# Block-sparse attention and an MLP on one core: a batch's last tile as one sparse and one dense unit, and the first chunk's down-projection in fp32

## The chip, the cores and the metric

The kernel runs on one core of a Trainium2 chip. A core has five engines that run side by side, each with its own list of instructions: TensorE (PE, matmuls; its weight loads are PEld), VectorE (DVE), ScalarE (ACT), GpSimd (POOL), and SyncE (SP), which issues DMAs. The metric is the device time in microseconds of one execution; the median of several runs is compared.

## What is computed

The reference is a block-sparse attention with a two-layer perceptron behind it, in fp32:

```python
scale = 1.0 / np.sqrt(D)
scores = scale * np.matmul(q, k.transpose(0, 1, 3, 2))
...
mask = np.abs(blk_i - blk_j) <= window
mask = mask | (blk_i == 0) | (blk_j == 0) | (blk_i == n_blocks - 1) | (blk_j == n_blocks - 1)
for qb in range(n_blocks):
    for kb in sampled_blocks[qb]:
        mask[qb * block:(qb + 1) * block, kb * block:(kb + 1) * block] = True
scores = np.where(mask, scores, -1000000000.0)
...
attn = attn / (np.sum(attn, axis=-1, keepdims=True) + 1e-09)
return np.matmul(attn, v).astype(np.float32)
...
h = x @ w_in
g = np.maximum(h, 0.0) + alpha * np.minimum(h, 0.0)
return (g @ w_out).astype(np.float32)
```

There are 4 batches, 8 heads, 768 tokens and 64 columns a head (D), so x has 3072 tokens of 512; w_in is 512 x 2048. `window` is 1, and three blocks are sampled for each of 24. A block is 32 tokens. A row of blocks 1 to 22 attends to at most eight blocks: itself and its neighbours, the first and the last, and three sampled ones. Rows of blocks 0 and 23 attend to all 24.

## The kernel before

**Numbers.** fp32 operands are split into a high and a low fp16 part, and a product is three fp16 matmuls (high x high, high x low, low x high). An fp32 matmul on unsplit operands gives the same product in one instruction that leaves two records in the trace. The weights come from memory as 64-bit numbers and are unpacked by bit operations on VectorE and ScalarE (`emit_n1`, `emit_n2`, `emit_n3`, L1151 to L1165) into fp32, 16 parts of w_in and 16 of w_out. Then squares on TensorE (`emit_w_sq`, L1175) and their diagonal (`emit_w_diag`, by `diag`, L547) give a scale, and `split` (L1274) makes the two fp16 parts: the high one by `times` (L451 on ScalarE), the low one by `rest` (L459 on VectorE, L461 and L462 on GpSimd). For the first five parts of w_out (`W_PE = 5`) the low part is made on TensorE instead (`emit_w_lo_pe`, L1237 and L1238) and copied out.

**Attention.** A batch has six query tiles of 128 rows, shifted by one block: tile t holds blocks 4t+1 to 4t+4, and the last one, t = TS = 5, blocks 21, 22, 23 and 0. The eight heads are two head sets of four. A unit u = (batch, tile, head set) is the work of one tile for one set. A *sparse* unit gathers its sampled keys (`emit_kr`, copies on GpSimd, L735) and values (`emit_vr`, indirect DMAs that GpSimd issues, L696), computes scores (`emit_s`), subtracts the maximum on VectorE (`emit_bias`, L822), takes exponentials on ScalarE, splits the probabilities, has them transposed by DMA from SyncE (`emit_p_t`, L872), and multiplies them by the values (`emit_av`). A *dense* unit takes all 768 keys: per head two halves of 384 (`emit_s_dense`) and 18 value matmuls (`emit_av_dense`). All matmuls of both kinds go through the helper `mm`, L740. Tiles 0 to 4 are sparse in both units, tile 5 is dense in both, because blocks 23 and 0 are in it. The tile's result is scaled, split (`emit_x_hi`, `emit_x_lo`) and transposed by one DMA (`emit_x_t`, L899) into `x`.

**The perceptron** takes chunks of 256 tokens, M0 to M11, three per batch. A chunk is eight up steps (`emit_up`, L1351, 24 fp16 matmuls of 256 columns), each with an activation on VectorE (`emit_act`, L1361 and L1365), a cast (`emit_gh`, L1374) and a low part (`emit_gl`, L1380), and eight down steps (`emit_down`, L1401, 12 fp16 matmuls of 512 columns). M0's up steps are fp32 on unsplit w_in (`emit_up32`, L1339), so that they need only the unpacked weights; its down steps use the split w_out.

**The order.** Every step is an operation of a plan, numbered as it is made. A list `ORDER` names all of them with a letter for the engine (P, D, A, G, S), and `Plan.run` emits them in just that order; dependencies without a semaphore then hold each engine to it. So each engine runs its list in order, and waits where an operand is late.

## Time and profile before

| | |
|---|---|
| median of 3 runs | 772.27 us (769.94 to 779.11) |
| profiled execution | 771.31 us, span 769.1 us, granted clock 0.982 |
| TensorE busy | 700.2 us, 91% |
| VectorE busy | 535.7 us, 70% |
| GpSimd busy | 483.1 us, 63% |
| ScalarE busy | 371.9 us, 48% |
| first and last matmul of the perceptron | 103.8 us, end at 764.6 us |

The span runs from the first to the last instruction of the profiled execution; 2.2 us of its time lie outside. "Busy" is the time in which an engine has at least one instruction under way. Granted clock is TensorE's, as a share of full speed. A label such as L740 is a line of the kernel, and for a helper all its callers share it.

### The profile page before, as it was taken

Reading aid. Unit: us, or ns where it says so; the run is one execution under the profiler, and the core shown is the slowest. Engines: PE = TensorE matmul, PEld = TensorE weight load, DVE = VectorE, ACT = ScalarE, POOL = GpSimd, SP = SyncE. Lnnn points to the kernel's source line nnn. Section 1 sums busy time; section 2 is a strip of 40 time slices with the busy share of each in tenths; the row PEclk is TensorE's granted clock in tenths of the full one; section 3 lists DMA queues with packets and bytes.
Section 4 is the critical chain, followed back from the end, with each engine's and each line's share of the span. In section 5 each row is a group of like instructions: output and inputs, shape, how many; then the busy total and the mean of one; then the engine's idle time right before and its main releaser. Section 6 shows DMA issues by size and latency. Waiting matters only on the chain.

```text
span 769.1 us, 25326 instructions
## 1 busy us (share of the span) xinstructions
PE 700.2 (91%) x9978; PEld 493.2 (64%) x9978; DVE 535.7 (70%) x1377; ACT 371.9 (48%) x838; POOL 483.1 (63%) x849
## 2 busy tenths in 40 slices
...
GB/s 180 326 276 208 204 171 236 164 178 144 163 185 227 173 200 201 207 202 194 174 197 197 208 182 218 186 188 172 185 213 199 150 155 162 167 99 113 65 1 29
DMA packets 284599, 136.49 MB, mean 177 GB/s; under 512 B 216992, under 2 KB 272304, under 8 KB 284480
## 3 DMA queue, kind: packets, MB, share of 16 engines
...
## 4 chain that ended last, share of the span: by engine, by line
PE 60%; DVE 16%; DMA 9%; issue 4%; POOL 4%; ACT 3%; SPq 2%; POOLq 0%; ACTq 0%; DVEq 0%
PE o L1401 24%; PE h L1351 23%; PE s L740 6%; PE a L740 5%; DMA pt<-ph 3%; DMA qs<-qt 3%; DVE ph L459 2%; DVE e L822 2%; POOL gl L1380 1%; DMA wo<-in_moe_w_in_dram 1%; DMA rawp<-in_sampled_blocks_dram 1%; DVE g L1361 1%; DVE wi L1165 1%; ACT rawp L447 1%; DVE wo L1165 1%
## 5 line engine op out<-in xcount | busy, mean ns | idle before, releaser
L1351 PE MATMUL h<-x,wi 128*128 128x256 f16 x2112 | 240.2, 273 | 0.7 <-DVE g L1365 0.7
L1351 PEld LDWEIGHTS <-wi 128*128 128x128 f16 x2112 | 204.7, 98 | 31.4 <-issue 2.2
L1401 PE MATMUL o<-wo,gh 128*128 128x512 f16 x728 | 219.7, 384 | 0.5 <-ACT g L1411 0.5
L1380 POOL TENSOR_TENSOR gl<-g,gh 128x512 f16<-128x512 f32 x91 | 110.5, 1221 | 90.6 <-ACT gh L1374 77.8
L735 POOL COPY keys<-keys 128x128 f16 x480 | 133.4, 327 | 20.6 <-ACT keys L604 16.1
L1401 PE MATMUL o<-wo,gl 128*128 128x512 f16 x364 | 139.7, 384 | 0.0
L829 ACT ACTIVATE e<-e,nm 128x256 f32<-128x256 f32 x160 | 79.9, 500 | 107.8 <-DVE nm L822 96.8
L1361 DVE SCALAR_TENSOR_TENSOR g<-h,am 128x512 f32<-128x512 f32 x96 | 65.9, 687 | 77.3 <-PE h L1351 57.0
L1401 PEld LDWEIGHTS <-gh 128*128 128x128 f16 x728 | 69.4, 99 | 77.8 <-issue 6.1
L1374 ACT CAST gh<-g 128x512 f16<-128x512 f32 x91 | 55.4, 611 | 105.1 <-DVE g L1365 57.6
L696 POOL DMA_INDIRECT vr<-scr,vidx x80 | 81.3, 1016 | 25.3 <-issue 19.8
L822 DVE CUSTOM_DVE_ANT_0 e<-s,bias,cs 128x256 f32<-128x256 f32 x160 | 73.5, 478 | 29.3 <-POOL ph L462 13.8
L1365 DVE SCALAR_TENSOR_TENSOR g<-h,gsc,g 128x512 f32<-128x512 f32 x96 | 72.1, 751 | 3.4
L740 PEld LDWEIGHTS <-pt 128*32 128x32 f16 (+1 forms) x4416 | 57.6, 96 | 25.0 <-issue 12.9
L740 PE MATMUL s<-keys,qs 128*32 128x192 f16 (+2 forms) x864 | 70.1, 255 | 2.9 <-DMA qs<-qt 2.9
L740 PE MATMUL s<-keys,qt 128*32 128x192 f16 (+2 forms) x864 | 69.4, 256 | 3.3 <-DVE nm L822 1.7
L1401 PEld LDWEIGHTS <-gl 128*128 128x128 f16 x364 | 35.9, 99 | 44.0 <-issue 1.9
L461 POOL TENSOR_SCALAR e<-e 128x512 f32<-128x512 f32 (+1 forms) x38 | 28.2, 742 | 57.1 <-ACT ph L451 24.8
L459 DVE SCALAR_TENSOR_TENSOR ph<-e,ph 128x512 f16<-128x512 f32 (+1 forms) x62 | 60.1, 975 | 4.2 <-ACT ph L451 3.7
L462 POOL TENSOR_TENSOR ph<-e,ph 128x512 f16<-128x512 f32 (+1 forms) x38 | 50.4, 1326 | 3.2
L451 ACT ACTIVATE ph<-e 128x512 f16<-128x512 f32 (+1 forms) x69 | 47.7, 693 | 9.3 <-DMA pt<-ph 8.1
L836 DVE CUSTOM_DVE_ANT_0 e<-s,dbias,cs 128x384 f32<-128x384 f32 x64 | 38.0, 612 | 11.2 <-PE s L740 8.1
...
## 6 DMA issues: line engine op xcount, KB each, us to landing
...
```

The lines of the kernel that those rows point to most:

```text
L459: nc.vector.scalar_tensor_tensor(dst, src, scale, hi, ALU.mult, ALU.subtract)
L696: nc.gpsimd.indirect_dma_start(dst[:n], None, T["scr", b].rearrange("s h a -> s (h a)"), bass.IndirectOffsetOnAxis(ap=vidx[:n, i : i + 1], ...
L735: nc.gpsimd.tensor_copy(kr[:, :, g, r], kt[:, :, bass.ds(i * HB2, HB2)])
L740: nc.tensor.matmul(dst, lhs, rhs, start=start, stop=False, skip_group_check=True)
L822: nc.vector.tensor_tensor_reduce(e_view(u, h // 2)[:, h % 2, :], T["sp", u, h], bias[:, t], scale=T["cs", b, t][:, c : c + 1], scalar=3.0e ...
L829: nc.scalar.activation(e, e, AF.Exp, bias=T["nm", u, h], scale=-1.0, accum_out=su_of(u, h))
L1351: nc.tensor.matmul(ph[:, i, :], win(k, f, ct), x[:, l, ct, cols], start=(m == 0), stop=(m == len(terms) - 1))
L1361: nc.vector.scalar_tensor_tensor(g, ph, 0.0, a2, ALU.min, ALU.mult)
L1365: nc.vector.scalar_tensor_tensor(g[:, i : i + 2], ph[:, i : i + 2], sc, g[:, i : i + 2], ALU.mult, ALU.add)
L1374: nc.scalar.copy(T["gh", c, j, half], g)
L1380: nc.gpsimd.tensor_tensor(T["gl", c, j, half], g, T["gh", c, j, half], ALU.subtract)
L1401: nc.tensor.matmul(T["o", c, t], g[:, i, a : a + P], wout(w, f), start=(f == 0 and m == 0), stop=(f == NF - 1 and m == 2),)
```

## The change

A batch's last tile becomes one sparse and one dense unit. Blocks 21 and 22 of all eight heads make the sparse one: rows 0 to 63 of the tile are the two blocks for the first head set, rows 64 to 127 the same blocks for the second. Blocks 23 and 0 of all eight heads make the dense one, in the same way. So the queries are loaded by six DMAs instead of two, scaled in two halves, and each dense matmul of 128 query rows becomes two of 64, one for each head set, that write different halves of the partitions (`row_sets`). `emit_x_t` puts the last tile back together with four transposes instead of one. The dense mask goes, since rows of blocks 23 and 0 attend to everything.

M0's down-projection becomes fp32 on unsplit w_out (`emit_down32`), in the order of steps 7 to 0, on the activations as they are: without `emit_gh` and `emit_gl` for that chunk. It needs the unpacked parts of w_out, and neither their scale nor their split. The split of w_out now stands behind these down steps, part by part, and all its low parts are made on VectorE or GpSimd. `ORDER` is a new list.

```diff
-W_PE = 5
...
-S289 S274 S26 A307 S272 S273 A308 D309 A312 D313 P12 D13 S290 G0 D1 D4 A8 S359 D27 A28 G2 S14 P275 D276 D277 P278 D279 S291 P314 P316 D29 A42 D317 S74
...
+S268 A269 D270 S251 A273 S250 D274 G0 D1 S25 S252 S193 S37 S194 S195 S29 D26 D27 D28 S17 S235 P253 D254 D255 D4 P277 A278 A9 D38 S233 D39 S320 A5 P256
...
+    NSB = NBLK - 2
+    HR = P // 2
...
     def emit_load_q(e, b, t):
         T["qf", b, t] = wt("qf", [P, H, D], F32)
+        if t == TS:
+            first = TS * P + BLK
+            for c in range(NQ):
+                hs = slice(c * HQ, (c + 1) * HQ)
+                for a, z, v, s in ((0, HR, 0, first), (0, BLK, 1, S - BLK), (BLK, HR, 1, 0)):
+                    load(e, T["qf", b, t][c * HR + a : c * HR + z, v * HQ : (v + 1) * HQ], q_tok[b][s : s + z - a, hs])
+            return
         for a, z, s in q_rows(b, t):
...
-    def picks(eng, t, use):
-        for i in range(NG4 * NR):
-            use(i // NR, i % NR, idx[eng][NG4 * NR * t + i])
+    def lay(u, g):
+        b, t, c = units[u]
+        return (c, g) if t < TS else (g // 2, g % 2)
+
+    def cs_of(u):
+        b, t, c = units[u]
+        return (c,) if t < TS else tuple(range(NQ))
...
+    def row_sets(u):
+        b, t, c = units[u]
+        return [(c, slice(0, P))] if t < TS else [(x, slice(x * HR, (x + 1) * HR)) for x in range(NQ)]
...
     def emit_s_dense(u, h, z):
-        b, t, c = units[u]
+        b, t, w = units[u]
         T["sp", u, h, z] = sp = wt("s", [P, 512], F32)
-        kt = T["kt", b, c][:, h, z]
         for x, key in enumerate(("qt", "qs")):
-            mm(sp[:, :CP], T[key, b, t][:, c * HQ + h, :], kt, x == 0)
+            for c, r in row_sets(u):
+                mm(sp[r, :CP], T[key, b, t][:, w * HQ + h, r], T["kt", b, c][:, h, z], x == 0)
...
     def emit_av_dense(u, h):
         b, t, c = units[u]
-        av = av_of(u) if h == 0 else T["av", b, t]
+        av = T["av", b, t]
         for i in range(NT):
-            av_mm(av[:, c * HQ + h], T["pt", u, h, i // 3], i % 3, v_tile(b, c, i, h), (c, h, i) == (0, 0, 0))
+            for x, y in TERMS:
+                for q, r in row_sets(u):
+                    mm(av[r, c * HQ + h], T["pt", u, h, i // 3][:, 3 * x + i % 3, r], v_tile(b, q, i, h)[:, y * D : (y + 1) * D], False)
...
+    def is_dense(u):
+        return units[u][1:] == (TS, 1)
...
     def emit_x_t(b, t):
         cc = chunks.index((b, t // 2))
         if ("x", cc) not in T:
             T["x", cc] = wt("x", [P, 2 * NC, W2], F16)
-        nc.sync.dma_start_transpose(
-            T["x", cc][:, :, (t % 2) * P : (t % 2 + 1) * P], T["xn", b, t].rearrange("p a c -> p (a c)")
-        )
+        x, xn = T["x", cc], T["xn", b, t]
+        if t < TS:
+            nc.sync.dma_start_transpose(x[:, :, (t % 2) * P : (t % 2 + 1) * P], xn.rearrange("p c l x -> p (c l x)"))
+            return
+        for w in range(2):
+            for c in range(NQ):
+                at = P + w * HR
+                nc.sync.dma_start_transpose(
+                    x[:, c * NC : (c + 1) * NC, at : at + HR], xn[c * HR : (c + 1) * HR, w * NC // 2 : (w + 1) * NC // 2].rearrange("p c l x -> p (c l x)")
+                )
 
...
-    def emit_w_lo_pe(name, f):
-        w, hi, lo, s = wparts(name, f)
-        T["d", name, f] = wt("o", [P, 512], F32)
-        nc.tensor.matmul(T["d", name, f], T["sid", f // 2 if name == "wi" else NG], w, start=True, stop=False)
-        nc.tensor.matmul(T["d", name, f], nident, hi, start=False, stop=True)
...
+    def split_all(name, o_w, free):
             if f == NF // 2:
                 prev = None
-            held = [o_al, o_pack] if f == 0 else []
-            prev, o_wi[f] = split("wi", f, 0, [gs[f // 2], ups[f // 2]] + held, prev, False, None, None)
+            prev = o_w[f] = split(name, f, free(f), prev)
...
+    def emit_down32(j):
+        if j == NG - 1:
+            for t in range(2):
+                T["o", 0, t] = wt("o", [P, DM], F32)
+        for i in range(2):
+            for t in range(2):
+                nc.tensor.matmul(
+                    T["o", 0, t], T["g", 0, j, None][:, i, t * P : (t + 1) * P], wo[:, 2 * j + i + 1, :],
+                    start=(j == NG - 1 and i == 0), stop=(j == 0 and i == 1),
+                )
...
+    def g_pool(c, j):
+        return "vf" if c == 0 and j < NG - bufs["g"] else "g"
...
-            sc = gsc[:, f : f + 1] if c else gsc0
+            sc = gsc[:, f : f + 1] if c else 1.0
...
+        if c == 0:
+            items = [("u", j) for j in range(ng)] + [("d", j) for j in reversed(range(ng))]
...
+                if c == 0:
+                    gh[j] = o
+                    continue
...
+            elif c == 0:
+                d = [gh[j]] + [raw_wo[n * j + i] for i in range(n)] + downs[-1:]
+                downs.append(plan.op(p, {"PE": 3.45}, lambda j=j: emit_down32(j), d, [] if downs else obufs, [gb[j]] + (obufs if downs else [])))
...
-            split_wi(ups)
+            split_all("wi", o_wi, lambda f: [gs[f // 2], ups[f // 2]] + [o_al, o_pack] * (f == 0))
+            split_all("wo", o_wo, lambda f: [o_swo, downs[NG - 1 - f // 2]])
...
-                if t < TS:
-                    gather(u, at(u - 3) if u > 2 else [])
-                    softmax(u, sparse_scores(u))
-                    sparse_values(u)
-                if t == TS:
+                if is_dense(u):
                     dense(u)
+                    continue
+                gather(u, at(u - 3) if u > 2 else [])
+                softmax(u, sparse_scores(u))
+                sparse_values(u)
```

Three places show how the instructions stand now. The first is VectorE around M0's first activation. Its rows in the kernel before (`e` are exponents, `s` scores, `cs` scales, `g` the activation, `h` the up step's result, `wo` an unpacked weight part); 254 rows stand ahead of the activation L1361:

```order
L822 ISA e_80,nm<-s_115,bias,cs 128x256
L822 ISA nm 128x1
L440 TENSOR_SCALAR uq<-ssq 128x1
L443 TENSOR_SCALAR sq<-uq 128x1
L822 ISA e_81,nm<-s_114,bias,cs 128x256
L822 ISA nm 128x1
L510 TENSOR_SCALAR cs<-rk,uq 128x1 x2
L822 ISA e_82,nm<-s_116,bias,cs 128x256
L822 ISA nm 128x1
L1361 SCALAR_TENSOR_TENSOR g_92<-h_119,am_185 128x512
L1365 SCALAR_TENSOR_TENSOR g_92<-h_119,gsc_186,g_92 128x512
```

In the changed kernel 226 rows stand ahead of the activation (L1363 there; `vf` is the buffer that it now goes to):

```order
L1172 TENSOR_SCALAR wo<-wo 128x512
L512 SCALAR_TENSOR_TENSOR qn_75<-qf_74,sq,qn_75 128x8x64
L1172 TENSOR_SCALAR wo<-wo 128x512
L1179 SCALAR_TENSOR_TENSOR wo<-wo 128x512
L1184 SCALAR_TENSOR_TENSOR wo<-wo 128x512
L430 SCALAR_TENSOR_TENSOR pt_83<-o_120,pt_83 128x2x256
L1363 SCALAR_TENSOR_TENSOR vf_69<-h_118,al 128x512
L1367 SCALAR_TENSOR_TENSOR vf_69<-h_118,vf_69 128x512
L501 TENSOR_SCALAR cs<-rk,uq 128x1
L1184 SCALAR_TENSOR_TENSOR wo<-x_89,wo 128x512
L1184 SCALAR_TENSOR_TENSOR wo<-wo 128x512
L1184 SCALAR_TENSOR_TENSOR wi<-wo,wi 128x512
```

Ahead of the activation stood three score evictions (L822, each with a row for its maximum) and small scalings; now one low part of transposed probabilities (L430) stands there, and weight unpackings (L1172 to L1184) on both sides.

The second is TensorE where M0's down-projection begins. Before, the last squares of w_out (L1175), their sum (L649) and the first of five low parts (L1237, L1238) stand between M0's ups and its first down step:

```order
L1175 LDWEIGHTS wo
L1175 MATMUL o_120<-wo 128x128
L1175 LDWEIGHTS wo
L1175 MATMUL o_120<-wo 128x128
L649 MATMUL o_121<-ident,otot 128x128
L1237 MATMUL o_120<-wo,sid_95 128x512
L1238 LDWEIGHTS nident
L1238 MATMUL o_120<-wo,nident 128x512
```

In the changed kernel the first down step (L1335) stands behind a sparse unit's scores (L739), and w_in's squares (L1194, L1201) follow it:

```order
L739 LDWEIGHTS qs_79
L739 MATMUL s_113<-keys,qs_79 32x2x96
L739 LDWEIGHTS qs_79
L739 MATMUL s_113<-keys,qs_79 32x2x96
L1335 MATMUL o_120<-wo,g_93 128x512
L1335 MATMUL o_119<-wo,g_93 128x512
L1335 MATMUL o_120<-wo,g_93 128x512
L1335 MATMUL o_119<-wo,g_93 128x512
L1201 MATMUL h_117<-isum,ones 128x1
L1194 LDWEIGHTS wi
L1194 MATMUL h_118<-wi 128x128
```

No square, sum or low part of w_out stands ahead of the down step any more.

The third is SyncE's list at the end of the program. Before, the last probabilities (`pt`) are followed by the last tile's transpose (of two tiles of `x`), and then the stores:

```order
L878 DMA_TRANSPOSE pt_84<-ph_138 128x6x128
L878 DMA_TRANSPOSE pt_83<-ph_138 128x6x128
L878 DMA_TRANSPOSE pt_86<-ph_139 128x6x128
L878 DMA_TRANSPOSE pt_85<-ph_139 128x6x128
L899 DMA_TRANSPOSE x_91<-xn_88 128x8x128 x2
L479 DMA out_dram<-g_92 128x512
L479 DMA out_dram<-g_94 128x512
```

In the changed kernel the last tile's transpose stands in four parts of 64 columns:

```order
L889 DMA_TRANSPOSE pt_83<-ph_139 128x6x128
L889 DMA_TRANSPOSE pt_85<-ph_139 128x6x128
L889 DMA_TRANSPOSE pt_84<-ph_137 128x6x128
L889 DMA_TRANSPOSE pt_86<-ph_137 128x6x128
L915 DMA_TRANSPOSE x_89<-xn_88 128x8x128
L920 DMA_TRANSPOSE x_89<-xn_88 128x4x64 x4
L450 DMA out_dram<-g_94 128x512
```

The whole-tile transpose of the tile before (L915) stays one row, the last tile's is four (L920), and each batch has six transposes of probabilities fewer (eight dense ones go, two sparse ones come).

## Rows read from the trace of the kernel before

**Rows 1.** Page, part 1: busy us, share of the span, instructions.
```profile
PE 700.2 (91%) x9978; PEld 493.2 (64%) x9978; DVE 535.7 (70%) x1377; ACT 371.9 (48%) x838; POOL 483.1 (63%) x849
```

**Rows 2.** Windows: three stages and the end; length, busy us by engine (instructions), clock, DMA.
```profile
0.00:103.80 103.80, 58.19 (x1006) 48.17 (x1006) 76.14 (x251) 54.16 (x100) 58.35 (x164) 0.95 0.77 231
103.80:292.00 188.20, 180.04 (x2425) 124.09 (x2421) 157.87 (x385) 113.16 (x248) 123.14 (x195) 0.97 0.87 187
292.00:764.60 472.60, 461.97 (x6556) 320.90 (x6552) 301.67 (x742) 203.79 (x490) 301.59 (x491) 0.99 0.84 162
764.60:769.10 4.50, 0.00 (x0) 0.00 (x0) 0.00 (x0) 0.76 (x2) 0.00 (x0) 0.94 0.35 118
```

**Rows 3.** Timeline, TensorE, 103 to 156 us: start, length, line, operation, out<-in, shapes, count.
```profile
103.77 7.17 PE L1339 MATMUL h<-x,wi 128*128 128x256 f32 x32
110.78 0.60 PE L632 MATMUL o<-ident,e 128*128 128x128 f32 x4
...
153.84 1.02 PE L1237 MATMUL o<-wo,sid 128*128 128x512 f32 x2
154.69 0.38 PE L1238 MATMUL o<-wo,nident 128*128 128x512 f16 x1
```

**Rows 4.** Chain that ended last, 252 to 262 us: start, length, instructions.
```profile
255.34 1.01 PE s L740 x40
...
259.07 0.91 PE a L740 x96
```

**Rows 5.** The same chain, 690 to 769 us.
```profile
697.53 0.33 PE s L740 x2
697.86 0.52 PE a L740 x18
...
715.14 7.77 PE o L1401 x36
722.91 13.10 PE h L1351 x120
...
746.43 2.59 PE o L1401 x12
749.02 2.62 PE h L1351 x24
```

**Rows 6.** Timeline, TensorE, 77 to 81 us.
```profile
77.60 0.63 PE L1175 MATMUL h<-wi 128*128 128x128 bf16 x8
78.07 0.61 PE L618 MATMUL o<-ident,qn 128*128 128x128 f16 x8
78.51 0.61 PE L632 MATMUL o<-ident,e 128*128 128x128 f32 x4
79.78 0.64 PE L621 MATMUL o<-ident,qn 128*64 128x128 f16 x16 [0.66 <-ACT qt L604]
80.34 0.38 PE L1182 MATMUL h<-isum,ones 128*128 128x1 f32 x2
```

**Rows 7.** Groups by line and form: busy us, mean ns of one | idle before, releaser.
```profile
L735 POOL COPY keys<-keys 128x128 f16 x480 | 133.4, 327 | 20.6 <-ACT keys L604 16.1 <-PE s L740 4.5
...
L696 POOL DMA_INDIRECT vr<-scr,vidx x80 | 81.3, 1016 | 25.3 <-issue 19.8 <-PE a L740 2.1 <-DVE wo L1165 1.2
...
L822 DVE CUSTOM_DVE_ANT_0 e<-s,bias,cs 128x256 f32<-128x256 f32 x160 | 73.5, 478 | 29.3 <-POOL ph L462 13.8 <-PE s L740 13.6 <-PE o L632 0.4
...
L1165 DVE SCALAR_TENSOR_TENSOR wi<-wo,wi 128x512 int32<-128x512 int32 x16 | 11.0, 708 | 0.0
...
L451 ACT ACTIVATE wo<-wo,s_wo 128x512 f16<-128x512 f32 x12 | 8.5, 717 | 8.1 <-DVE wo L459 6.9 <-PE o L1237 1.0 <-DVE wo L453 0.2
...
L459 DVE SCALAR_TENSOR_TENSOR wo<-wo,s_wo 128x512 f16<-128x512 f32 x9 | 8.1, 901 | 0.8 <-ACT wo L451 0.8
```

**Rows 8.** Instructions on tile x: count, ns min/median/max, first and last start.
```profile
L899 SPq DMA_TRANSPOSE x<-xn x22: 1231/1243/1822, 151.6 to 717.8; - x22
```

**Rows 9.** DMA issues by tile: count, median us from issue to landing.
```profile
x<-xn SPq DMA_TRANSPOSE x22, 4.6
```

473 lines of the change are left out of this document (220 added, 253 removed).

## The prediction

> **What bounds the kernel now.** I read the page first: TensorE is busy 91% of the 769.1 us span, VectorE 70%, GpSimd 63% [rows 1]. So the end is set by TensorE, but that is an average. The windows, cut where the first up-projection starts (103.8 us) and where the fourth chunk's starts (292.0 us), show three stages [rows 2]. In the first VectorE works 76.1 of 103.8 us, and nothing of the perceptron can start. In the second TensorE and VectorE are both loaded: 157.9 us of VectorE in 188.2 us. In the third, 472.6 us long, TensorE is busy 462.0 us and VectorE only 301.7; there the sum of TensorE's work is the time, nearly. Busy time hides gaps below an instruction's length, so I counted the work too: instructions times the pitch at which they follow one another in the timeline and in the chain that ended last [rows 3 to 5]. That gives 171.2 us of TensorE work for the second stage (a share of 171.2 / 188.2 = 0.91) and 453.2 us for the third (19.4 us are lost there). Behind them come 4.5 us without TensorE [rows 2].
>
> **The prices, from rows.** An fp32 up-projection pair: 32 records in 7.01 us (to the next row's start at 110.78) are two of eight, 3.50 us each. An fp32 matmul of 512 columns takes 0.85 us (153.84 to 154.69) [rows 3]; the new down step is four of them, 3.4 us, as many columns as an up step's eight of 256 in 3.50, so I take 3.45 us. A sparse unit's scores take 1.01 us and its values 0.91 us [rows 4]. An fp16 down step is 2.59 us, an up step 2.62 us, a dense half-head's scores (two matmuls) 0.33 us, and a dense head's values (18 matmuls) 0.52 us [rows 5]. A norm (8 matmuls) is 0.47 us (77.60 to 78.07) [rows 6].
>
> **The dense unit.** A batch's last tile had two dense units; it now has one sparse and one dense one. Per batch that removes 8 half-head scores (2.6 us) and 4 heads' values (2.1 us), and adds 1.01 + 0.91 us: -2.8 us, four times, -11 us. This holds only if the two halves of 64 query rows, which now follow one another as 64-column matmuls, run side by side, since their number has not fallen. No row shows it for these operands. The nearest are transposes: 16 of 64 columns start 0.56 us before their successor, 8 of 128 columns 0.44 us [rows 6]. So a pair takes 70 ns where a full one takes 55: mostly side by side. Groups of four 32-column matmuls do it fully (96 in 0.91 us, 38 ns a group) [rows 4]. I take the halved price; the lower bound is nothing lost, the upper no overlap, 10.6 us of scores and 8.3 us of values more, 18.9 us. On the side, VectorE loses half of the 64 dense score evictions and gains 16 of 0.48 us; GpSimd gains 48 copies of 0.327 us (15.7 us) and 8 gathers of 1.0 us [rows 7], and loses 8 splits of g and some of the dense low parts. It stays near 483 us in all.
>
> The Trainium skill (TensorEngine Tiling, Restrictions and Gotchas) says that column tiling excludes fast weight load, and (TensorE: Matmul & The Clock Gate, LDWEIGHTS) that a load takes its columns over 1.2 GHz. By that 36 loads of 64 columns would take an estimated 1.9 us a head, not 0.52, and the sum would be about 22 us higher; the trace's 32-column groups speak against it, and no run here shows 64-column ones of this kind.
>
> **The down-projection of the first chunk.** Removed: eight fp16 down steps (20.7 us), five low parts of w_out made on TensorE (0.85 + 0.22 us each, 5.4 us), eight casts on ScalarE and eight subtractions on GpSimd. Added: eight fp32 steps, 27.6 us. TensorE: +1.5 us. So it saves nothing in work; what it moves is the waiting. It needs raw w_out only, not the norm of all of w_out and the split, which now stand behind it. GpSimd and VectorE take over the five low parts (0.90 us each on VectorE) [rows 7].
>
> **The order, first stage.** Ahead of the first activation on VectorE, 7 unpackings fewer of each of two kinds (the longer one 0.71 us [rows 7]; two more of a third), 6 fewer norm diagonals, 6 fewer scales, 6 fewer score evictions and some copies stand: 17.8 us by mean times count. Successive instructions overlap (all groups by mean times count add to 599 us, the page has 535.7), so that is 17.8 x 0.894 = 16 us. VectorE was idle 27.7 us in this stage (103.8 less 76.1 [rows 2]); I keep that idle time, because the attention chain that causes it is the same. The first up-projection then starts at 103.8 - 16 = **87.8 us**. Bounds: none of it, if the chain alone sets the start, or a few us more.
>
> **Second stage.** It holds all of chunks 0, 1 and 2's ups: 8 fp32 ups 28.0, 16 ups 41.9, 16 downs 41.4, 8 fp32 downs 27.6, 13 scores and 11 values of sparse units 23.2, 8 dense scores and 4 values 4.7, 13 norms 6.1 (7 before) and small things 5.5: **178.4 us** against 171.2, which had 24 downs. VectorE's list comes to 173.2 us against 157.7 (the trace has 157.9, so the counting holds). At the same share of 0.91 the stage lasts 178.4 / 0.91 = **196 us** and ends at 283.8, not 292.0. VectorE would be at 88% there, 84% before; that is the tight place.
>
> **Third stage.** 72 ups and downs stay. Three last tiles lose 14.1 us of dense work and gain 5.8, and 1.1 us has moved ahead: 453.2 becomes **443.8 us**. With the same 19.4 us lost: 463.2.
>
> **The last transposes.** The last tile's x now goes out as four transposes. SyncE issues one in 1.24 us or so, and x lands 4.6 us from its issue; now it was issued at 717.8, 2.7 us behind the last values (715.14), and the ups began at 722.91, right behind three downs that hid it [rows 5, 8, 9]. Three more issues of 0.3 to 1.24 us put the landing 0 to 3.3 us behind the same three downs, which stand there still. In the other batches other chunks' work hides it, and without that cover it costs the same again. I take 2.5 us, since the issue time is the same for the smaller transposes of probabilities.
>
> **Sum.** 283.8 + 463.2 + 2.5 + 4.5 = 754.0 us of span. The profiled execution took 771.3 us for its 769.1 us of span, 2.2 us around it; its time lies 1 us below the median of 772.27. Forecast: 756, and with a little less queueing at SyncE (24 transposes of probabilities fewer) **755 us**, 2.2% below the median. About 2% (15 us) is what a measurement of this kernel can tell from no change: the line is at 757.
>
> **Rivals.**
> - *The second stage packs better.* Long fp32 matmuls need little from others: each down step waits for one activation alone. At 0.95 it lasts 187.8 us, 8 less: **747**. For it: the stall for the norm and split is gone. Against: VectorE would have to work 92% of the time.
> - *VectorE takes the place of TensorE there.* At its own share of before, 157.9 / 188.2 = 0.839, its 173.2 us need 206 us, 10 more: **765**. For it: the two lists run level all the way to the third chunk, so each late split stops TensorE. Against: no row says that 0.839 is all it can do; it was idle there for TensorE, which ended the stage.
> - *The halves of the dense unit do not overlap*, so it costs what both did: 755 + 18.9 = **774**. The transposes speak against it; the skill's page above gives something near.
> - *Slower: the split of w_out lands on the path.* Its 16 parts (0.72 us on ScalarE, then 0.90 on VectorE [rows 7]) can be made only after the down step that reads the raw part, and now stand behind chunk 1's fifth up. If they run in that order with nothing beside, 16 x 1.62 = 26 us come between chunk 1's ups and its first down: 755 + 26 = **781**, slower than before. It decides from 17 us of delay on. Against: 27 us of TensorE work (seven ups, a unit and half) lie between the last fp32 down and that first fp16 down; VectorE has 27 us in the same place, so lateness passes through one for one.
>
> **Chances.** Forecast (748 to 762) 0.45, better packing 0.20, VectorE 0.20, no overlap 0.08, split on the path 0.07. The likeliest is 755. The range reaches from 742 to 774 and leaves out the last case and the edge of the second. Faster by over 2%: all of the second case and some 0.27 of the first, 0.47. Slower by over 2% (above 788): the worse part of the last case, 0.05. Within 2%: 0.48.
>
> **What would show it.** The first fp32 up at 85 to 91 us; the fourth chunk's first up near 284; fp32 downs at 3.45 us a step with no gap above 1 us between the last up and the first down; a dense half-head at 0.33 us and a dense head's values at 0.52 to 0.65; a third stage of about 465 us. I am wrong if the first up comes near 100 us, if TensorE waits for w_in's or w_out's split around chunk 1, or if waits for GpSimd's key copies grow in chunk 2, where its list (67 us) exceeds TensorE's (62).

## The result, and the profile after

The changed kernel takes **781.95 us** (median of 18 runs, 778.17 to 786.36) against 771.31 us for the kernel before (18 runs, 766.94 to 779.11): a ratio of 1.0142, interval 1.0114 to 1.0169. The forecast was 755 us, 2.2% faster; it came out 1.4% slower, outside the range. Its profiled execution took 785.83 us, 3.9 us above the median, and has a span of 784.0 us; the control run below (a_ctl, profiled at 780.75 us) shows how much of each stage repeats.

The page's first part, as [rows 1]: busy time, share of the span, instructions.

```profile
PE 701.2 (89%) x10507; PEld 486.0 (62%) x10507; DVE 523.1 (67%) x1337; ACT 349.4 (45%) x831; POOL 467.4 (60%) x876
```

VectorE, ScalarE and GpSimd have 12 to 23 us less to do than in [rows 1], TensorE 1 us more, and every share is lower: all engines wait more. The windows, cut as [rows 2] at the first up-projection, at chunk 3's first up and at the last matmul (length, busy us by engine, granted clock, DMA share, GB/s):

```profile
0.00:86.80 86.80, 47.29 (x873) 39.15 (x873) 61.73 (x198) 46.33 (x94) 48.03 (x141) 0.93 0.82 235
86.80:298.60 211.80, 188.78 (x2694) 130.84 (x2690) 164.96 (x428) 106.82 (x245) 133.67 (x228) 0.96 0.84 180
298.60:779.40 480.80, 465.14 (x6944) 316.01 (x6944) 296.39 (x713) 195.47 (x491) 285.71 (x508) 0.98 0.82 158
779.40:784.00 4.60, 0.00 (x0) 0.00 (x0) 0.00 (x0) 0.73 (x2) 0.00 (x0) 0.76 0.35 116
```

| | first up at | second stage | third stage | end | sum |
|---|---|---|---|---|---|
| before [rows 2] | 103.8 | 188.2 | 472.6 | 4.5 | 769.1 |
| forecast | 87.8 | 196.0 | 463.2 + 2.5 | 4.5 | 754.0 |
| after | 86.8 | 211.8 | 480.8 | 4.6 | 784.0 |

The first stage is right to 1 us. The second is 16 us longer than forecast and ends at 298.6 us, 6.6 us *later* than before, though the perceptron began 17 us sooner. The third is 15 us longer than forecast (in the control 211.6 and 478.3 us, so 16 and 13 us). Finer windows of the second stage, after and then before, show where TensorE stands still:

```profile
86.80:122.40 35.60, 35.60 (x441) 30.57 (x437) 29.01 (x64) 15.52 (x29) 16.39 (x35) 0.97 0.75 206
122.40:158.90 36.50, 36.50 (x438) 19.66 (x436) 30.91 (x97) 20.53 (x51) 25.07 (x38) 1.00 1.07 216
158.90:209.00 50.10, 48.38 (x790) 35.49 (x790) 46.64 (x120) 30.95 (x62) 27.99 (x26) 1.00 0.81 150
209.00:240.00 31.00, 30.03 (x308) 20.72 (x309) 24.83 (x60) 19.91 (x52) 23.10 (x56) 1.00 0.74 165
240.00:298.60 58.60, 38.27 (x731) 24.40 (x726) 33.58 (x91) 19.92 (x54) 41.12 (x74) 0.87 0.81 176
```

```profile
239.50:292.00 52.50, 52.50 (x845) 36.34 (x843) 33.97 (x91) 21.74 (x60) 44.11 (x81) 1.00 0.91 195
```

Up to 240 us TensorE is busy 150.5 of 153.2 us, 98%; before it was 96% over the whole stage [rows 2]. From 240 us to chunk 3's first up it is idle for 20.3 of 58.6 us, and its granted clock is 0.87. Before, chunk 2's stretch of the same place had no idle TensorE at all: 52.5 of 52.5. VectorE has the same work there, 33.6 against 34.0 us, and GpSimd 3 us less. So the work is not more; what TensorE needs comes late.

The waits of TensorE from 240 to 298.7 us (engine, line, waited for: us in total, times, longest) name four kinds; the same view of before, over 240 to 292.1 us, has no line:

```profile
PE s L739 <- DVE nm L825: 7.3, 3, 3.7
PE a L739 <- DMA vn<-scr: 6.9, 1, 6.9
PE h L1350 <- DMA x<-xn: 4.5, 1, 4.5
PE h L1350 <- DVE g L1367: 1.6, 1, 1.6
```

What stands behind these 20.3 us can be read from the queues; this is a reading, and e_order and e_fix below test part of it. ScalarE's timeline: the DMAs of neighbour values for unit 13 (`vn<-scr`, ACTq) stand behind an exponential that waits 8.86 us for VectorE.

```profile
264.17 0.51 ACT L832 ACTIVATE e<-e,nm 128x256 f32<-128x256 f32 x1 [8.86 <-DVE nm L825]
264.22 0.33 ACTq L450 DMA_DIRECT2D vn<-scr  x1
```

SyncE's timeline: the group of `vn<-scr` that starts at 249.67 lasts 25.09 us. Four of its six DMAs are issued by 252.5 us; the last two need the buffer that unit 13's values free, and go out from 273.26 us. Three transposes of probabilities stand behind them until 274.86.

```profile
247.56 2.02 SPq L885 DMA_TRANSPOSE pt<-ph  x1
249.67 25.09 SPq L450 DMA_DIRECT2D vn<-scr  x6
274.86 4.02 SPq L885 DMA_TRANSPOSE pt<-ph  x3
```

GpSimd's timeline: it waits 3.68 and 3.23 us, and then 24 copies of keys (7.54 us) and four gathers stand ahead of the low part of x (L907) that chunk 3 needs.

```profile
274.84 1.16 POOL L907 TENSOR_TENSOR xn<-xf,xn 128x512 f16<-128x512 f32 x1 [3.68 <-ACT xn L902]
279.23 1.16 POOL L1377 TENSOR_TENSOR gl<-g,gh 128x512 f16<-128x512 f32 x1 [3.23 <-ACT gh L1372]
280.34 7.54 POOL L736 COPY keys<-keys 128x128 f16 x24
...
293.75 1.18 POOL L907 TENSOR_TENSOR xn<-xf,xn 128x512 f16<-128x512 f32 x1
```

The third stage. TensorE's longest waits there, after and then before:

```profile
PE h L1350 <- DMA x<-xn: 12.6, 7, 4.5
PE h L1350 <- DVE g L1367: 3.3, 1, 3.3
```

```profile
PE a L740 <- DMA pt<-ph: 6.3, 6, 1.9
PE s L740 <- DMA qs<-qt: 2.9, 2, 2.6
PE h L1351 <- DVE g L1365: 0.7, 1, 0.7
```

After, x itself is late at the start of chunks (4.5 of the 12.6 us lie just ahead of chunk 3's first up and belong to the second stage, 8.1 to the third). Behind the longest of these waits the clock is down: the ups from 472.0 to 478.4 us run at a granted clock of 0.53, just above the lower level of 1.2 GHz, after 4 us without a matmul. The same holds behind the 4.5 us ahead of chunk 3 (0.59 from 298.6 to 305.0 us) and behind the 3.3 us for an activation (0.55 from 430.5 to 434.0); behind the waits for x of 1.5 us and less (ups from 405.6, 574.0 and 737.7 us) it is 1.00.

```profile
468.00:472.00 4.00, 0.00 (x0) 0.00 (x0) 0.00 (x0) 0.92 (x3) 0.45 (x2) 0.90 1.25 151
472.00:478.40 6.40, 6.38 (x32) 4.64 (x32) 2.22 (x5) 2.02 (x5) 1.77 (x2) 0.53 1.29 194
```

The same 1728 up matmuls are busy 203.78 us after and 196.48 before (windows of that line alone, in the third stage). So late operands cost twice: in waiting, and in 7.3 us of slow ups behind the longer waits. Against before, the stage has 3.2 us more busy time (465.1 for 462.0) and 5.0 us more idle time (15.7 for 10.6).

### The profile page after: what moved, and what is told of

Its sections match the earlier page's. It is cut to its first block, busy times and chain, and to the rows that moved or that the text cites. A ratio compares the mean times of both kernels' runs of the same rounds, so it can differ in the third digit from the quotient of the medians.

```text
span 784.0 us, 26438 instructions
## 1 busy us (share of the span) xinstructions
PE 701.2 (89%) x10507; PEld 486.0 (62%) x10507; DVE 523.1 (67%) x1337; ACT 349.4 (45%) x831; POOL 467.4 (60%) x876
## 4 chain that ended last, share of the span: by engine, by line
PE 66%; DVE 7%; DMA 7%; issue 7%; POOL 6%; ACT 3%; SPq 2%; POOLq 1%; ACTq 0%; DVEq 0%
PE h L1350 25%; PE o L1398 20%; PE s L739 6%; PE a L739 5%; PE h L1327 4%; PE o L1335 4%; DMA x<-xn 3%; POOL keys L736 2%; SPq L920 2%; POOL vr L690 1%; DVE ph L430 1%; DMA vr<-scr,vidx 1%; DMA rawp<-in_sampled_blocks_dram 1%; POOL gl L1377 1%; DVE e L825 1%
## 5 line engine op out<-in xcount | busy, mean ns | idle before, releaser
L1350 PE MATMUL h<-x,wi 128*128 128x256 f16 x2112 | 248.0, 278 | 19.3 <-DMA x<-xn 14.3
L1398 PE MATMUL o<-wo,gh 128*128 128x512 f16 x704 | 212.5, 384 | 0.0
L736 POOL COPY keys<-keys 128x128 f16 x528 | 143.2, 320 | 43.8 <-PE s L739 19.0
L832 ACT ACTIVATE e<-e,nm 128x256 f32<-128x256 f32 x176 | 87.8, 499 | 120.3 <-DVE nm L825 110.3
L1363 DVE SCALAR_TENSOR_TENSOR g<-h,am 128x512 f32<-128x512 f32 x88 | 60.4, 686 | 79.2 <-PE h L1350 64.6
L825 DVE CUSTOM_DVE_ANT_0 e<-s,bias,cs 128x256 f32<-128x256 f32 x176 | 80.2, 477 | 33.6 <-PE s L739 23.4
L739 PE MATMUL s<-keys,qt 128*32 128x192 f16 (+2 forms) x960 | 63.9, 254 | 10.3 <-DVE nm L825 7.9
L739 PEld LDWEIGHTS <-pt 128*32 128x32 f16 (+1 forms) x4800 | 51.5, 99 | 30.6 <-issue 25.2
L430 DVE SCALAR_TENSOR_TENSOR ph<-e,ph 128x512 f16<-128x512 f32 (+1 forms) x62 | 54.4, 883 | 19.0 <-ACT ph L422 18.5
L739 PE MATMUL s<-keys,qs 128*32 128x192 f16 (+2 forms) x960 | 64.1, 252 | 0.0
L432 POOL TENSOR_SCALAR e<-e 128x512 f32<-128x512 f32 (+1 forms) x30 | 21.7, 722 | 50.6 <-DVE ph L424 31.2
L739 PE MATMUL a<-vn,pt 128*32 128x64 f16 x2112 | 41.6, 200 | 7.3 <-DMA vn<-scr 6.9
L739 PE MATMUL a<-vr,pt 128*32 128x64 f16 x2112 | 42.2, 200 | 3.9 <-issue 1.9
L739 PEld LDWEIGHTS <-qt 128*32 128x32 f16 (+2 forms) x960 | 37.2, 101 | 12.9 <-issue 7.8
```

The costliest lines, as they stand in the source:

```text
L430: nc.vector.scalar_tensor_tensor(dst, src, scale, hi, ALU.mult, ALU.subtract)
L736: nc.gpsimd.tensor_copy(kr[:, :, g, r], kt[:, :, bass.ds(i * HB2, HB2)])
L739: nc.tensor.matmul(dst, lhs, rhs, start=start, stop=False, skip_group_check=True)
L825: nc.vector.tensor_tensor_reduce(e_view(u, h // 2)[:, h % 2, :], T["sp", u, h], bias[:, t], scale=T["cs", b, t][:, c : c + 1], scalar=3.0e ...
L832: nc.scalar.activation(e, e, AF.Exp, bias=T["nm", u, h], scale=-1.0, accum_out=su_of(u, h))
L1350: nc.tensor.matmul(ph[:, i, :], win(k, f, ct), x[:, l, ct, cols], start=(m == 0), stop=(m == len(terms) - 1))
```

## The experiments

Theories, by the letters that the expectations use. **A**: the next batch's attention is a chain over queues that are served in order, and it sets when chunk 3 can start. **B**: TensorE's sum of work sets it, as the prediction took it. **C**: VectorE's sum does. **D**: the DMA engines are nearly full, and late landings set it. Later, inside A: **G** (GpSimd's list), **V** (VectorE's list in one stretch), **O** (the order in which ready and late work stand on the queues), **P** (GpSimd keeping VectorE waiting). The runs stand on several chips, so they are read mainly by intervals between the first ups of chunks (M0 to M11), from their traces:

| kernel | M0 at | M0 to M1 | M1 to M2 | M2 to M3 | M3 to end | ratio to before |
|---|---|---|---|---|---|---|
| before | 103.8 | 67.7 | 68.0 | 52.5 | 472.6 | 1 |
| after | 86.8 | 74.8 | 47.5 | 89.5 | 480.8 | 1.0142 [1.0114, 1.0169] |
| a_ctl | 84.4 | 74.8 | 47.2 | 89.6 | 478.3 | 1.0147 [1.009, 1.0203] |
| e_thin | 91.5 | 73.1 | 46.8 | 88.2 | 484.8 | 1.0115 [1.0023, 1.0207] |
| e_nolo | 91.1 | 75.1 | 45.9 | 92.4 | 495.3 | 1.0322 [1.0248, 1.0397] |
| e_order | 91.8 | 75.1 | 47.4 | 85.8 | 491.7 | 1.0296 [1.0221, 1.037] |
| e_xt1 | 94.5 | 75.2 | 46.8 | 92.6 | 487.2 | 1.0282 [1.0207, 1.0357] |
| b_thin | 106.1 | 65.8 | 73.3 | 54.2 | 470.9 | 1.0005 [0.9964, 1.0045] |
| e_hold | 85.4 | 73.9 | 48.5 | 87.2 | 478.1 | 1.0122 [1.0082, 1.0162] |
| a_thin3 | 84.8 | 74.0 | 47.2 | 91.3 | 470.8 | 0.9987 [0.9954, 1.0019] |
| e_gp | 85.8 | 74.0 | 47.5 | 87.8 | 474.3 | 1.0067 [1.0026, 1.0108] |
| e_vlo | 85.5 | 73.8 | 47.6 | 89.3 | 478.3 | 1.0099 [1.0061, 1.0137] |
| d_st | 86.7 | 74.2 | 47.0 | 89.8 | 477.9 | 1.0068 [1.0026, 1.0109] |
| e_fix | 88.0 | 75.4 | 47.5 | 82.0 | 479.1 | 1.0041 [0.9992, 1.0089] |
| p_port | 86.5 | 75.0 | 47.3 | 88.8 | 476.6 | 1.0146 [1.0104, 1.0188] |
| e_both | 85.9 | 75.1 | 47.5 | 83.4 | 477.2 | 1.0028 [0.9985, 1.007] |

**a_ctl**, the changed kernel again, beside e_hold, a_thin3 and b_thin on one chip.

> The changed kernel itself, as a control on the chip and in the rounds of the next three. Expected as recorded: 1.014 of the kernel before, first up of chunk 3 about 298 us, and 20 us of idle TensorE between 240 and 298 us. A chip on which it differs by more than 1% from that would say that the earlier four trials have to be read against their own first-up times and not against the recorded median.

784.09 us; chunk 3 at 296.0 us. It repeats the result, and the intervals to within 0.3 us up to chunk 3. The four trials e_thin, e_nolo, e_order and e_xt1 ran on another chip, with first ups at 91.1 to 94.5 us and no control beside them; their intervals are used, and they are compared with one another. e_gp, e_vlo, d_st and e_fix ran on a third chip together, p_port and e_both later on the same; "the control" is a_ctl for them too.

### Is it a sum of work?

**e_thin** leaves out 28 of the 32 fp32 down matmuls of the first chunk.

```diff
-        for i in range(2):
+        for i in {NG - 1: (0,), 0: (1,)}.get(j, ()):
```

> Changed kernel without 28 of the 32 fp32 matmuls of the first chunk's down-projection (only the first and the last pair stay, so the output is not the product); 28 x 0.85 = 23.9 us of TensorE work less between 122 and 159 us, same lists otherwise. Theory A (the fourth chunk's start is set by the preparation of the second batch's attention, which runs over several in-order lists, not by TensorE's work): the second chunk starts 10 to 24 us earlier than 161.6, the fourth chunk's first up stays within 6 us of 298.6, the time is 774 to 784. Theory B (TensorE's work sets the second stage, the fp32 steps cost too much): the fourth chunk's first up 20 to 24 us earlier, the time 758 to 763.

The second stage of e_thin, by windows:

```profile
91.50:299.60 208.10, 169.27 (x2638) 123.74 (x2634) 164.81 (x431) 107.24 (x247) 134.99 (x228) 0.93 0.88 181
```

TensorE is busy 19.5 us less than in the changed kernel (169.27 for 188.78), and the stage lasts 208.1 us instead of 211.8; in e_nolo and e_xt1, on the same chip and with all downs, it lasts 213.4 and 214.6. So 4 to 6.5 us came out, and the larger part of the work that was taken away turned into idle time. Theory B falls for the changed kernel as a sum, though not to nothing. Theory A missed something too: it had chunk 1 10 to 24 us earlier, and it came 1.7 us earlier (73.1 for 74.8). The median, 790.5 us, lies 12 to 16 us below those of the other three trials on this chip (802.4 to 806.4); without a control it stays open how much of that is the thinning.

**b_thin** asks the same of the kernel before: the first chunk's 96 fp16 down matmuls work on 64 columns instead of 512.

```diff
+                    z = DM if c else 64
...
-                        T["o", c, t],
+                        T["o", c, t][:, :z],
...
-                        wout(w, f),
+                        wout(w, f)[:, :z],
```

> The kernel before with the first chunk's 96 fp16 down matmuls cut from 512 to 64 columns (all dependencies stay): about 16 us less TensorE work in the second stage, from 20.7 us (96 at 0.216) to some 4. If the second stage of before was bound by TensorE's sum, as the prediction took it, chunk 3's first up comes 16 us earlier. If the chain of the attention set it there too, chunk 3 moves by under 4 us, and the prediction's 196 us for the second stage was wrong already for the kernel before.

```profile
106.10:299.40 193.30, 170.17 (x2426) 121.12 (x2422) 153.50 (x385) 113.14 (x248) 123.68 (x196) 0.92 0.86 182
```

The second stage is 193.3 us long instead of the 188.2 of [rows 2], with TensorE busy 170.2 us instead of 180.0, and the time is unchanged (1.0005 [0.9964, 1.0045]; the kernel before ran beside it). So TensorE, busy 180.0 of 188.2 us, was not the bound of that stage even before. Part of what was removed comes back as a slower clock (0.92 for 0.97): TensorE now stands idle in between, 23.1 us for 8.2.

**e_nolo** fills the low parts of w_out with zeros (`memset` for a subtraction), which should take some 10 us out of VectorE's list; in the stage VectorE is busy 157.3 us for 165.0.

```diff
+        if name == "wo":
+            (nc.vector if e == "DVE" else nc.gpsimd).memset(lo, 0.0)
+            return
```

> Changed kernel in which the 16 low parts of w_out (15 of them on VectorE, 0.9 us each) are filled with zeros instead of being computed, so some 10 us of VectorE work go between 160 and 240 us. Theory C (VectorE's sum of work sets the second stage): the fourth chunk's first up 9 to 12 us earlier than 298.6, the time 770 to 773. Theory A (a chain of waits over several lists sets it): 2 to 7 us earlier, the time 775 to 780. Theory B (TensorE's work): no change, 780 to 784.

Chunk 1 to chunk 2 is 1.6 us shorter than after, chunk 2 to chunk 3 is 2.9 us longer, and the stage is 213.4 us long (e_xt1, on the same chip, 214.6). VectorE's sum over the stage is not the bound; theory C falls. Its third stage, 495.3 us, is the longest of the four on that chip; why stays open.

**a_thin3** leaves one of the twelve matmuls of each up unit out, in chunks 3 to 11.

```diff
+            if c > 2:
+                terms = terms[:5] + terms[6:]
```

> The changed kernel with one of the twelve matmuls of each up-projection unit left out in chunks 3 to 11: 16 per chunk, 144 in all, at 0.112 us each 16 us less TensorE work in the third stage. If the third stage is bound by TensorE's sum, as the prediction took it, the stretch from chunk 3's first up to the last matmul shortens by 16 us. If it is bound by the chain of the attention, it shortens by under 5 us and TensorE is idle for the rest. In between: the share of the 16 us that comes out is the share of the stage in which TensorE is the bound.

Its third stage, and that of the control:

```profile
297.30:768.10 470.80, 450.19 (x6800) 302.03 (x6800) 296.67 (x711) 194.45 (x489) 286.13 (x507) 0.98 0.84 161
```

```profile
296.00:774.30 478.30, 463.75 (x6944) 315.78 (x6944) 298.60 (x713) 195.45 (x491) 286.39 (x508) 0.98 0.84 159
```

Of 13.6 us less busy time, 7.5 us come out in the profile, and 11.8 us between the medians (784.09 to 772.33). So in the third stage TensorE's sum is worth 55% to 87% of its size. There theory B holds in the main.

### Is it one resource?

**e_hold**: five of the first chunk's eight groups, those whose activations lie in the buffers for batch 1's loads, have no activation and no down-projection (the same two lines stand in both steps).

```diff
+        if g_pool(0, j) == "vf":
+            return
```

> The changed kernel with five of the eight groups of the first chunk left without activation and without down-projection (the five whose activations lie in the buffers that batch 1's keys and values are loaded into). That takes out 15 us of TensorE work, which an earlier trial has shown to be worth nothing, about 6 us of VectorE, and the wait of batch 1's loads for those buffers. Theory A (the next batch's attention runs as a chain over queues served in order, and what makes it late is the hold on the load buffers until the fp32 downs have run): the first up of chunk 3 comes 8 to 12 us earlier than in the control, and the total falls by as much. Theory D (the DMA engines are nearly always busy, so that landings are late whatever is issued when): the loads start earlier but chunk 3 moves by less than 3 us.

Chunk 3 came 1.0 us earlier than in the control (chunk 2 to chunk 3 2.4 us shorter). The trace shows why this settles little: batch 1's key loads went out at 139.8, 144.9 and 148.8 us, in the control at 138.8, 144.6 and 148.2. Freed of the buffer, they still stood in SyncE's list where they stood. The hold is not what delays chunk 3 in this order; whether it would in another stays open. Under 3 us is what the expectation gave to theory D; d_st tests that.

**e_vlo** cuts the low parts of v, in batches 1 to 3, from 64 columns to 8 (and clears one buffer at the start).

```diff
-            rest(e, v2[:, a, :, 1, :], src[:, a], ...)
+            z = 8 if b else D
+            rest(e, v2[:, a, :, 1, :z], src[:, a, :, :z], ...)
```

> The changed kernel with the low parts of v cut, in batches 1 to 3, from 64 columns to 8 (0.55 us each to some 0.15, two per tile and set, the number of instructions stays; the rest of the low part is old data). That takes 4 to 5 us out of VectorE's list between 209 and 248 us, where it is busy 94% and the chain of waits runs on it without a break from 227 to 246 us. Theory V (VectorE's list is the bound in this stretch, though its sum over the stage is not): chunk 3 comes 3 to 5 us earlier, and the total falls by 3 to 10. If another queue ends last there, under 1.5 us.

No interval moved: 89.3 us from chunk 2 to chunk 3, 478.3 behind. Theory V falls.

**d_st** stores only 64 of 512 columns.

```diff
-            load(e, out[b * S + s : b * S + s + z - a], T["ob", c, t][a:z])
+            load(e, out[b * S + s : b * S + s + z - a, :64], T["ob", c, t][a:z, :64])
```

> The changed kernel that stores only 64 of the 512 columns of its output: 24 stores of 256 KB fall to 32 KB, so about 5.5 MB of the DMA traffic goes, and no dependency and no instruction changes. From the DMA section of the profile (q10: 9.6 MB take 8.3% of 16 engines over 460 us, 4 us per MB) that is an estimated 2 to 3% of the DMA engines' time. Theory D (the DMA engines, busy 82 to 87% throughout, are the real bound or make every landing late): the time falls by 1.5 to 3%, 12 to 24 us. If the DMA engines only matter where one landing is waited for: under 5 us.

Second and third stage by windows; the last two columns are the DMA share and GB/s:

```profile
86.70:297.70 211.00, 187.05 (x2694) 130.03 (x2690) 166.79 (x428) 106.57 (x245) 133.92 (x228) 0.96 0.81 177
297.70:775.60 477.90, 463.64 (x6944) 315.89 (x6944) 299.02 (x713) 195.38 (x491) 286.29 (x508) 0.98 0.78 151
```

The share fell by 3 and 6 points against the control, as wanted, and the two stages are 211.0 and 477.9 us long, where the control has 211.6 and 478.3. The ratio is lower by 0.8 points, the median by 3 us (781.01 for 784.09, on another chip); no stretch of the traces shows either. The 12 to 24 us of theory D did not come; a few us are not excluded. As the bound of the kernel, DMA engines that are busy four fifths of the time are out.

**e_gp** cuts GpSimd's copies of picked keys from eight planes to one, in batches 1 to 3.

```diff
-                nc.gpsimd.tensor_copy(kr[:, :, g, r], kt[:, :, bass.ds(i * HB2, HB2)])
+                z = 1 if b else kr.shape[1]
+                nc.gpsimd.tensor_copy(kr[:, :z, g, r], kt[:, :z, bass.ds(i * HB2, HB2)])
```

> The changed kernel with GpSimd's copies of picked keys cut, in batches 1 to 3, from eight planes to one (the number of instructions stays; the scores of those batches then use old keys in seven of eight planes). 396 copies at 0.320 us fall to 0.1 to 0.15 us (an estimate): some 9 us less GpSimd work between 228 and 288 us, and about 75 us less over the whole kernel. If GpSimd's list sets chunk 3 (theory G: the chain before it runs over low part of g, copies of keys, gathers, low part of x), its first up comes 5 to 9 us earlier, near 289, and the total falls by 10 us or more, since the later batches have the same list. If not, under 3 us at chunk 3.

GpSimd's work fell by 40 us over the last two stages, not by 75. Chunk 2 to chunk 3 is only 1.8 us shorter than in the control, but chunk 5 to chunk 6 is 60.6 us for 66.7. So GpSimd's copies matter in one place of the third stage, and little at chunk 3. The time fell by 0.8 points. VectorE's busy time in the third stage fell too, from 298.6 us to 284.0, though none of its work was taken away.

**e_xt1** issues the last tile's x as one transpose instead of four.

```diff
-        if t < TS:
+        if True:
```

> Changed kernel in which a batch's last tile is transposed by one DMA as the other tiles are (its rows then hold a wrong mix of heads, the output of those tokens is not the reference's), so three SyncE issues of 1.2 us fewer per batch. If the four transposes cost at each batch's end, as the waits of TensorE for x ahead of chunks 3, 6, 9 and 12 say (1 to 3 us each): the time 773 to 777. If they cost only at the very end, where nothing hides them: 778 to 780. If they are hidden: 781 to 783.

In its last chunk the ups follow the three downs without a wait. In the changed kernel that wait is 0.23 us: SyncE's three more issues of 1.25 us are nearly hidden by the downs (chain that ended last, after).

```profile
728.14 1.28 PE a L739 x72
...
737.72 3.34 PE h L1350 x29
```

The other batches show more. Over the whole changed kernel TensorE's ups wait 5.8 us, in 7 times, for the four transposes (the view of line L920): 1.7 us ahead of chunk 2, 2.1 ahead of chunk 5, 1.7 ahead of chunk 8 and 0.2 ahead of chunk 11, the chunks that hold a batch's last tile; the control has 5.6 us. In e_xt1 none of these waits is left. The waits ahead of chunks 3 and 6, which the expectation had in mind, are for other tiles, and stay. Chunk 4 to chunk 5 takes 55.4 us for 57.3 in the control; what the four transposes cost in all is not shown, for want of a control on that chip.

### Is it the order?

**e_order** moves three entries of the table: unit 13's neighbour values on ScalarE ahead of the exponentials (A887), unit 15's on SyncE behind transposes (S938), and GpSimd's gathers for unit 16 behind the low part of x (G970).

```diff
-... A948 G762 ... P885 A887 P903 S938 ... S928 P773 ... G970 ... G958 ...
+... A948 A887 G762 ... P885 P903 ... S928 S938 P773 ... G958 G970 ...
```

> Changed kernel with three operations moved in the order list and nothing else: the load of the near values of the second batch's second unit goes ahead of two waits for VectorE in ScalarE's list, a load that waits for its buffer goes behind two transposes of probabilities in SyncE's list, and four gathers go behind the low part of x in GpSimd's list. Theory A: TensorE's gap of 6.9 us ahead of that unit's values shrinks below 2 us, the fourth chunk's first up comes 5 to 10 us earlier than 298.6, the time is 772 to 778. Theories B and C (the sum of TensorE's or VectorE's work): the start moves by less than 2 us, the time is 780 to 784.

Chunk 2 to chunk 3 fell by 3.7 us to 85.8 (e_xt1, on the same chip, has 92.6). The 6.9 us wait for `vn<-scr` was gone; 4.2 us of "issue" waits of TensorE and GpSimd's copies of keys were next. Its time is no better than those of e_nolo and e_xt1 beside it.

**r_before, r_tile, r_down, r_after**: the kernel before, the last tile alone, the fp32 down-projection alone, and both, each with a whole new order table, found by a search over durations taken from the traces, in a model without contention.

> The kernel before with the same operations in another order: the order list was searched anew with each operation's duration taken from the two traces. If the order that each kernel came with is what separates them, all four reordered kernels (before, last tile alone, down-projection alone, both) are compared on equal terms: by the sums of TensorE's work this one should be the slowest of the four, with both 9 to 20 us faster than it. If the change costs by itself, this one is the fastest. Time by the model 712 to 760; the model has no contention, so the upper part is likelier: 745.

> The kernel before with the change of the last tile alone (one sparse and one dense unit), down-projection as before, order searched in the same way. If the last tile's work sets the time, as the sum said (11 us of TensorE less): 8 to 14 us faster than the reordered kernel before. If the gain is eaten by GpSimd's extra copies and gathers: within 3 us of it.

> The kernel before with the fp32 down-projection of the first chunk alone, last tile as before, order searched in the same way. By the sum it saves nothing in TensorE's work (1.5 us more) and moves the wait for w_out's split: 0 to 8 us faster than the reordered kernel before. If fp32 costs by itself: 2 to 8 us slower.

> The changed kernel, both parts, same operations in an order searched in the same way. If the order is what lost the gain (theory A): faster than the changed kernel by over 3% and faster than the reordered kernel before by 9 to 20 us; by the model 694, on the chip 730 or so. If the change itself costs: slower than the reordered kernel before.

They took 822.55, 840.99, 818.43 and 850.88 us: ratios of 1.0605, 1.0899, 1.0556 and 1.1021. The expectations were missed, by 78 us for r_before (745) and by 121 for r_after (730). The same arithmetic as the kernel before costs 6% more in an order that such durations call good. Within these four the tile adds 18 us, the down-projection takes 4 off, and both together add 28; since each order is bad in its own way, this says nothing sure about the parts. What it shows is the size of the order's effect, and where it bites. TensorE's longest waits in r_after are all landings:

```profile
PE a L739 <- DMA pt<-ph: 17.0, 8, 9.5
PE a L739 <- DMA vn<-scr: 14.6, 3, 6.1
PE a L739 <- DMA vr<-scr,vidx: 13.3, 6, 6.2
```

**e_fix** moves three entries of the changed kernel's table, chosen from the three timelines above, and changes no work: A887 and S938 as in e_order, and GpSimd's copies of keys for unit 18 (G1020) into its waiting time.

```diff
-... A948 G762 ... P885 A887 P903 S938 ... S928 P773 ... G919 D964 ... P778 G1020 G1039 ...
+... A948 A887 G762 ... P885 P903 ... S928 S938 P773 ... G919 G1020 D964 ... P778 G1039 ...
```

> The changed kernel with three instructions moved in the order table, no work changed: on ScalarE's queue the copy of neighbour values for unit 13 (A887) goes ahead of the exps behind which it stood 9 us after its data had landed; on SyncE's queue the same copy for unit 15 (S938) goes behind the transposes that were held up by it; on GpSimd the copies of keys for unit 18 (G1020) go into the 3 us in which it waits for the perceptron, ahead of the low part of g. Theory O (the order: late instructions ahead of ready ones): chunk 3 comes 4 to 8 us earlier measured from chunk 2's first up, and the total falls by 3 to 8. If it gains at chunk 3 and the total does not move, the gain is lost again further back, where the order was laid out for other times. If nothing moves, the order in this stretch is not the cause.

Chunk 2 to chunk 3 fell by 7.6 us (82.0 for 89.6), and the time to 775.27 us, 1.0041 for 1.0147: about 8 us by the ratios, 5 to 6 against p_port and e_vlo on the same chip (780.3 and 781.5), with not one instruction added or removed. Theory O holds for these us: chunk 3 waited for a few late instructions by their place in the lists.

**p_port** moves two casts of probabilities from VectorE to ScalarE.

```diff
-... A1467 D1468 P1474 ... D2194 D2201 S2188 ...
+... A1467 A1468 P1474 ... D2194 A2201 S2188 ...
```

> The changed kernel with two instructions moved from VectorE to ScalarE in the order table (the high parts of probabilities of units 26 and 44, D1468 and D2201; ScalarE is idle there), no work changed. In the trace of the changed kernel and of its control the first of them takes 6.4 and 7.1 us on VectorE where the median of its line is 0.44, while GpSimd runs 23 copies of keys and a low part of g back to back beside it; with the copies shrunk (e_gp) the outlier is gone and chunk 6 comes 6 us earlier. Theory P (VectorE's instruction is kept waiting by GpSimd's, and an activation behind it stops TensorE for 3.3 us at 427 us, with half clock behind): the interval from chunk 5's first up to chunk 6's falls by 4 to 6 us, from 66.7 to about 62, and the total by 4 to 7 us. If the delay was not on the path: under 1.5 us at chunk 6.

This is the second place, in chunk 5. VectorE's timeline of the changed kernel, and GpSimd's beside it:

```profile
422.65 6.43 DVE L424 TENSOR_SCALAR ph<-e 128x512 f16<-128x512 f32 x1 [0.67 <-ACT e L832]
429.00 0.67 DVE L1363 SCALAR_TENSOR_TENSOR g<-h,am 128x512 f32<-128x512 f32 x1
```

```profile
420.94 4.77 POOL L736 COPY keys<-keys 128x128 f16 x20
425.68 1.15 POOL L1377 TENSOR_TENSOR gl<-g,gh 128x512 f16<-128x512 f32 x1
426.78 3.16 POOL L736 COPY keys<-keys 128x128 f16 x12
```

The same instruction in e_gp, where the copies are small:

```profile
418.17 0.43 DVE L424 TENSOR_SCALAR ph<-e 128x512 f16<-128x512 f32 x1 [0.67 <-ACT e L833]
```

It takes 0.43 us there and 6.43 here, 7.07 in the control, beside GpSimd instructions that follow one another without a pause. Behind it the activation (L1363) is late, and TensorE waits 3.3 us for it. With the cast on ScalarE, chunk 5 to chunk 6 falls by 3.6 us, from 66.7 to 63.1; the next VectorE instruction with two operands is now held up instead:

```profile
422.49 3.71 DVE L430 SCALAR_TENSOR_TENSOR ph<-e,ph 128x512 f16<-128x512 f32 x1
```

Theory P is shown as a mechanism, with most of its size; but the time did not fall (1.0146 for 1.0147). 1.3 of the 3.6 us were lost again by chunk 7 (46.7 us for 45.4) and 1.4 behind it (260.8 us from chunk 7's first up to the last matmul for 259.4), and its first up came 2.1 us later than the control's, of which 1.3 were won back by chunk 5.

**e_both** joins e_fix and p_port, and puts the last transposes of x for chunk 6 ahead of a copy of neighbour values (S1494 ahead of S1524).

```diff
-... S1524 A1560 D1493 S1855 S1494 S1857 ...
+... A1560 D1493 S1855 S1494 S1524 S1857 ...
```

> The three moves of e_fix, the two of p_port, and on SyncE the last transposes of x for chunk 6 ahead of the copy of neighbour values behind which they stood 1.4 us (S1494 ahead of S1524); no work changed against the changed kernel. If the order is the cause (theory O), the gains add: 7.6 us from chunk 2 to chunk 3, 4 to 6 us from chunk 5 to chunk 6, and the total comes to 769 to 772 us, level with the kernel before or a little below. If lateness only passes on to the next place where the order was laid out for other times, it stays at e_fix's 775.

774.4 us, 1.0028 for 1.0147: 9 us by the ratios, 6 against p_port on the same chip, won by six moved entries, and level with the kernel before, not below it. Chunk 3 starts at 291.9 us; chunk 5 to chunk 6 takes 60.2 us, 6.5 less than in the control; but chunk 6 to chunk 7 takes 50.8 instead of 45.4, 5.4 us back. So the gains of e_fix and of the second place did not add up: lateness was partly passed on to the next place, as the expectation's second case has it. Its second and third stage:

```profile
85.90:291.90 206.00, 190.32 (x2694) 131.16 (x2690) 163.04 (x426) 106.58 (x245) 132.74 (x227) 0.97 0.89 183
291.90:769.10 477.20, 458.72 (x6944) 312.96 (x6944) 292.43 (x712) 196.37 (x493) 287.16 (x508) 0.99 0.82 160
```

## Why the prediction was wrong

**The first stage** was right: 86.8 us for 87.8. VectorE is busy 14.4 us less there (61.7 for 76.1, 16 counted) and idle 2.6 us less (kept in the forecast), so the size comes from the term that was named. That VectorE's list is what sets the first up was not tested.

**The prices of the new steps** were right or nearly so. An fp32 down step is 3.54 us (eight records, 153.0 to 156.5 us in the control) for 3.45. The halves of the dense unit do run side by side. A half-head's scores are now four matmuls of 64 rows; its four matmuls stand in two rows, and the next half-head starts at 707.68:

```profile
707.33 0.35 PE L739 MATMUL s<-keys,qt 128*64 128x384 f16 x2
707.52 0.33 PE L739 MATMUL s<-keys,qs 128*64 128x384 f16 x2
707.68 0.33 PE L739 MATMUL s<-keys,qt 128*64 128x384 f16 x2
```

That is 0.35 us a half-head (707.33 to 707.68) for the 0.33 of [rows 5]. A head's values, 36 matmuls, take 0.64 us in the chain above (72 in 1.28) for 0.52: 0.12 us more a head. So the rival of no overlap, 774 us, was not what happened. Nor was the 1.9 us a head that the prediction estimated from the Trainium skill's rule that column tiling excludes fast weight load (TensorEngine Tiling (Array Packing), Restrictions and Gotchas), with 36 loads one behind the other: the trace does not agree with that estimate, and the measurement decides. Two counts were too high: VectorE's work in the second stage (165.0 us for 173.2) and GpSimd's in all (467.4 us for "near 483").

**The last transposes** were forecast to cost 2.5 us behind chunk 3's start, at the very end above all. There they cost 0.23, because the three downs hide them. But ahead of chunks 5 and 8 TensorE waits 2.1 and 1.7 us for them: 4.0 us of waiting in the third stage, half of its 8.1 us for x, and 1.7 us more in the second. The condition "without that cover it costs the same again" was the one that came true.

**The step that failed** is the sentence "At the same share of 0.91 the stage lasts 178.4 / 0.91 = 196". It takes the 0.91 for TensorE's own, as if the stage were TensorE's work stretched a little. b_thin and e_thin show that it is an outcome: with TensorE busy 10 us less before, the stage is 5 us longer and the time the same; with 19.5 us less after, the stage is 4 us shorter. By the traces, what ends the stage is the moment at which batch 1's first two tiles have gone through scores, exponentials, transposes, values and x. Chunk 3 began at 292.0 us before, and at 291.9 to 300.1 us in every trial on the changed order but e_nolo and e_xt1 (304.5 and 309.1): a first stage 17 us shorter did not bring it forward. It is no fixed moment: in those two the first up is 7 to 10 us later than in the control, and chunk 3 is 8.5 to 13 us later. What did not come forward with the change is batch 1's attention. Its six loads of keys are issued from 113.9 to 190.3 us before and from 141.2 to 197.8 after, the last of its six loads of values at 226.1 and 228.1. The last one before, and the first and the last after:

```profile
226.14 0.53 SPq L479 DMA_DIRECT2D vf<-in_v_dram  x1
```

```profile
141.17 0.54 SPq L450 DMA_DIRECT2D vf<-in_k_dram  x1
...
228.11 0.37 SPq L450 DMA_DIRECT2D vf<-in_v_dram  x1
```

Before, TensorE had a backlog of perceptron to fill that time, and was busy 52.5 of 52.5 us in the last stretch. Now the perceptron is ahead, the backlog is spent by 240 us, and the 17 us come back as 20.3 us of idleness. The forecast moved the perceptron forward and left out that the next attention, whose x it needs, had not moved.

Within that, e_fix shows that the place of three late instructions in the new table was worth 7.6 us. It does not show what all 89.5 us between chunk 2 and chunk 3 hang on; the rest of the chain was only read, in the trace. None of the prediction's three signs of being wrong came: the first up was at 86.8 us, and TensorE waits neither for a split nor directly for key copies around chunks 1 and 2. The third sign was the nearest: key copies stood on GpSimd ahead of the low part of x.

**The rivals.** Better packing was right up to 240 us and then worth nothing. "VectorE takes the place of TensorE" gave 765 us for a second stage of 206; the stage is longer (211.8), but not by VectorE's sum (e_nolo, e_vlo). The slower rival, w_out's split on the path, gave 781 us; that it comes within 1 us of the 781.95 measured is luck, since its mechanism is not there: the fp32 downs run on from the ups with no idle TensorE (36.5 of 36.5 us from 122.4 to 158.9), and there is no wait for the split.

**The third stage** was given "the same 19.4 us lost" on 443.8 us. Two terms failed, besides the transposes. The saving in attention is real on its own lines: the matmuls of scores and values are busy 77.52 us, before 87.65 (windows of these lines alone). But in e_both, whose granted clock in that stage is 0.99 as before, all of TensorE is busy 458.7 us for 462.0: 3.3 us less, of the 9.4 forecast. The dearer values explain 0.12 x 12 = 1.4 us of the difference. Most of the rest lies where lines of the kernel overlap on TensorE: busy line by line they add up to 484.8 us before and 474.1 in e_both, 10.7 less, but 22.8 and 15.4 us of that lie side by side. Why less overlaps stays open. And the loss is not a constant: x is late six times in the stage, 8.1 us, an activation once, 3.3 us, and ups behind the longer waits run at a lower clock, 7.3 us. e_gp, p_port and e_both show one cause of it, ahead of chunk 6: GpSimd's copies beside VectorE, and SyncE's order.

**What stays open**: why the order that goes with the change is late there at all, and whether a good order for the changed work would be faster than before. The kernel with six moved entries is level with the kernel before.
